# Weight conversion in 8 rounds with its last pass on GpSimd, and the first eight attention slots taken by token tile and turned on TensorE

## The chip, the cores and the metric

One core of a Trainium2 chip runs the whole kernel. The metric is device time in microseconds for one execution: 929.83 is the median of three runs of the kernel before, which lie between 923.97 and 930.18. The profile is of one more execution, timed at 926.31.

PE is the matrix engine (TensorE), DVE is VectorE, ACT is ScalarE, POOL is GpSimd, and SP is the engine whose queue issues most transfers. Matrix products land in PSUM, which GpSimd does not touch in this kernel; everything else is in the on-chip memory SBUF.

## What is computed

```python
scores = scale * np.matmul(q, k.transpose(0, 1, 3, 2))        # 8 batches, 8 heads, 576 x 576, depth 64
thresh = np.max(scores, axis=-1, keepdims=True) - tau
scores = np.where(scores >= thresh, scores, -1e9)
attn = exp(scores - max);  attn = attn / (sum(attn) + 1e-9)
x = matmul(attn, v)           # heads side by side: 4608 tokens x 512
h = x @ w_in                  # 512 x 1024
sm = softmax(h);  solu = h * sm
ln = (solu - mean) / sqrt(var + 1e-6) * g_ln
out = ln @ w_out              # 1024 x 512
```

q, k and v are 32-bit floats. The two weight matrices are 64-bit floats, and the kernel makes 32-bit floats of them with integer operations on the two words of each number.

## The kernel before, in words

**Slots and rounds.** A slot is one pair of heads with 128 queries of one batch. There are 18 slots to a batch: for each of two halves of the queries (`kind` 0 and 1) and each head pair `hp`, the two groups `r` of 128 queries; then two slots for the last 64 queries. The main loop runs one round per slot, 144 in all, and then some rounds of feed-forward alone. A round issues, in this order written out by hand, the scores of its slot on PE (L391, two PSUM tiles `s0`, `s1`, one for each head of the pair), the row maxima with the threshold on DVE (L408), the threshold ramp on ACT (L419), the exponentials with their sums on ACT (L428), and then for the slot before it `normalise` on GpSimd (L435 to L438: one over the sum, times each row) and `blocks` on DVE (L450: 32 x 32 block transposes into `T`). After both slots of a head pair four transfers on SP's queue (L461) bring the blocks into `wT`, and three or four rounds after that `attend` (L486) multiplies by v. Engines take their instructions in the order of issue, so what is issued later in a round stands behind what came earlier.

**Queries and keys.** q and k arrive with tokens on partitions. `whole_pair` turns one head pair of batch 0 with products by the identity into both PSUM tiles `p0` and `p1`, and six copies (`keep`, L297, L322, L338, L342) bring it to SBUF; it does so before round 0 and in rounds 0, 2 and 4. Later pairs are turned item by item in the spare columns of the score tiles. The keys are stored in an order of columns that suits the transposes of the weights (`k_parts`).

**Feed-forward.** When all head pairs of 256 tokens are attended, two tiles of 128 tokens become ready. A tile takes a cycle of four rounds, a quarter each: two halves of the first product (`ff_h`, L540, with a marker on GpSimd, `fence`, L106, between them), and in the next two the two halves of the second product (`ff_o`, L642) of the tile before. Between them come the softmax and the norm on ACT, DVE and GpSimd (L553 to L609), four transfers (L620) and a transpose on DVE (L630). The second product also waits until all weights are there (`w2_done`). Tiles 0 and 1 of batch 0 need slots 0 to 7, tiles 2 and 3 slots 8 to 15.

**Weights.** There are sixteen pieces of 128 x 512 numbers, eight of `w_in` and eight of `w_out`. In rounds 0 to 15 one piece is converted per round: the exponent (L216) and the mantissa (L222) are cut out on DVE, ACT puts the exponent in place (L221), and DVE then adds the low word (L236), puts in the sign (L239) and multiplies the two parts and the unit (L242). A piece of `w_out` is also copied with its partition halves exchanged (L251). Three buffers hold raw pieces; the next one is requested (L205) when its buffer's piece is done.

## Time and profile before

| | us |
|---|---|
| median of three runs | 929.83 |
| the profiled execution, as timed | 926.31 |
| its span | 924.5 |
| PE busy / DVE / ACT / POOL | 854.7 / 679.0 / 592.0 / 452.8 |
| L408, row maxima, mean of one | .755 |
| L428, exponential, mean of one | .772 |
| L438, scaling of one head's rows on GpSimd, mean of one | .771 |
| L436, reciprocal of the sums on GpSimd, mean of one | .745 |
| L236, L239, L242, passes of a weight piece on DVE | .656, .679, .692 to .752 |
| L216, L222, exponent and mantissa on DVE | .452, .479 |
| L221, exponent on ACT | .727 |

Busy times are sums over instructions of one engine; a mean is over all its instructions of that line. In the rows that the prediction shows, the first number of a row in order of time is its start from the beginning of the span and the second its duration, both in us; the square bracket says how long the engine was idle before it and what it waited for. In rows of groups the count stands after x, then the busy time in us and the mean of one in ns, then idle time before them. In the view of forty slices each digit is the busy share of a slice in tenths.

### The profile page before, as it was taken

The numbers are of one execution on the slowest core, as the hardware profiler recorded it, in microseconds if no ns is written. First come the engines' busy times: TensorE is split into PE (matmuls) and PEld (weight loads), VectorE is DVE, ScalarE is ACT, GpSimd is POOL, SyncE is SP. The second block draws the span as 40 slices with busy tenths as digits, with TensorE's granted clock in tenths as the row PEclk, the third lists the DMA queues.
The fourth block names the chain that finished last, engine by engine and source line by source line (L and its number), as shares of the span: only waits on it lengthen the run. The fifth ranks groups of instructions, "written<-read, shape, count | busy, mean of one in ns | idle before, by whom it ended". The sixth has DMA issues, their size and how long they took to land. (4 is left out here: it accounts for less than half of the span.)

```text
span 924.5 us, 39657 instructions
## 1 busy us (share of the span) xinstructions
PE 854.7 (92%) x17089; PEld 624.7 (68%) x17089; DVE 679.0 (73%) x1306; ACT 592.0 (64%) x1240; POOL 452.8 (49%) x870
## 2 busy tenths in 40 slices
PE   4657779989999999989997999999999999999997
...
DVE  4998967768867877767876777767877777877352
...
GB/s 244 200 260 261 186 124 198 229 179 124 187 169 224 128 140 185 237 150 134 184 183 209 94 136 182 229 150 130 186 185 224 121 131 128 191 145 140 90 47 47
DMA packets 95470, 154.61 MB, mean 167 GB/s; under 512 B 27192, under 2 KB 69184, under 8 KB 95296
## 3 DMA queue, kind: packets, MB, share of 16 engines
...
## 5 line engine op out<-in xcount | busy, mean ns | idle before, releaser
L408 DVE CUSTOM_DVE_ANT_0 w<-s_ps,tau_t 128x576 f32<-128x576 f32 x288 | 206.6, 755 | 157.2 <-PE s_ps L391 133.8
L419 ACT ACTIVATE w<-s_ps,nth 128x576 f32<-128x576 f32 x288 | 207.6, 744 | 127.1 <-DVE nth L408 106.2
L642 PE MATMUL o_ps<-w,uT 64*64 64x256 f32 x4608 | 271.2, 380 | 11.3 <-DVE uT L630 9.0
L642 PEld LDWEIGHTS o_ps<-w,uT 64*64 64x64 f32 x4608 | 221.6, 134 | 70.6 <-issue 27.9
L438 POOL TENSOR_SCALAR w<-w,sm 128x576 f32<-128x576 f32 x288 | 218.6, 771 | 14.3
L428 ACT ACTIVATE w<-w,ntau 128x576 f32<-128x576 f32 x288 | 220.3, 772 | 0.0
L540 PE MATMUL h_ps<-w,xh 64*64 64x512 f32 x1856 | 218.0, 591 | 0.7 <-issue 0.7
L450 DVE STREAM_TRANSPOSE T<-w 128x576 f32<-128x576 f32 x288 | 205.8, 751 | 4.5 <-POOL w L438 4.2
L486 PEld LDWEIGHTS pv<-wT,v 64*64 64x64 f32 x5760 | 168.0, 137 | 44.1 <-issue 24.7
L391 PE MATMUL s_ps<-kT,qT 64*64 64x64 f32 (+1 forms) x2048 | 173.2, 425 | 22.5 <-ACT w L419 19.0
L486 PE MATMUL pv<-wT,v 64*64 64x128 f32 (+1 forms) x5760 | 171.2, 265 | 10.8 <-DMA wT<-T 8.3
L540 PEld LDWEIGHTS h_ps<-w,xh 64*64 64x64 f32 x1856 | 110.1, 134 | 93.3 <-issue 67.9
L435 POOL TENSOR_SCALAR sm<-sm 128x2 f32<-128x2 f32 x144 | 36.1, 251 | 275.7 <-ACT w L428 272.9
L436 POOL TENSOR_TENSOR sm<-sm,mone 128x2 f32<-128x2 f32 x144 | 107.2, 745 | 12.0
L391 PEld LDWEIGHTS s_ps<-kT,qT 64*64 64x64 f32 x2048 | 64.1, 139 | 34.9 <-ACT w L419 24.9
L604 ACT ACTIVATE V<-u,nb,rs 128x1024 f32<-128x1024 f32 x36 | 44.7, 1241 | 53.2 <-POOL nb L594 53.2
L508 ACT COPY xh<-pv 128x256 f32<-128x256 f32 x64 | 23.9, 374 | 68.1 <-PE pv L486 68.1
L630 DVE STREAM_TRANSPOSE uT<-V 128x1024 f32<-128x1024 f32 x36 | 44.1, 1224 | 23.9 <-DMA V<-u 23.9
L562 ACT ACTIVATE u<-h_ps,hm 128x1024 f32<-128x1024 f32 x36 | 40.3, 1118 | 26.4 <-DVE hm L553 20.8
L428 ACT ACTIVATION_READ_ACCUMULATOR w<-w,ntau 128x1 f32 x288 | 57.0, 198 | 0.0
L553 DVE TENSOR_REDUCE hm<-h_ps 128x1 f32<-128x1024 f32 x36 | 43.0, 1195 | 9.4 <-PE h_ps L530 6.0
L568 DVE TENSOR_TENSOR u<-h_ps,u 128x1024 f32<-128x1024 f32 x36 | 42.8, 1189 | 9.6 <-ACT u L562 9.6
...
## 6 DMA issues: line engine op xcount, KB each, us to landing
wT<-T SPq DMA_DIRECT2D x288, 288.0 KB, 5.7
V<-u SPq DMA_DIRECT2D x144, 64.0 KB, 3.8
...
```

Of the source, the lines that this page charges most:

```text
L391: nc.tensor.matmul(out=ps[h][ROWS[y], ks], lhsT=lhsT, rhs=d["kT"][ROWS[h], ks], start=True, stop=True,)
L408: nc.vector.tensor_tensor_reduce(out=w, in0=ps[:, 0:S], in1=tau_t.to_broadcast([P, S]), scale=1.0, scalar=BIG, op0=ALU.add, op1=ALU.min, a ...
L419: nc.scalar.activation(out=d["w"][x], in_=d["ps"][x][:, 0:S], func=AF.Prelu, bias=d["nth"][x], scale=-1.0, alpha=1.0e30,)
L428: nc.scalar.activation(out=w, in_=w, func=AF.Exp, bias=ntau, scale=1.0, accum_out=sm[:, x : x + 1])
L436: nc.gpsimd.tensor_tensor(out=sm, in0=sm, in1=mone, op=ALU.pow)
L438: nc.gpsimd.tensor_scalar(out=w, in0=w, scalar1=sm[:, x : x + 1], scalar2=1.0, op0=ALU.mult, op1=ALU.mult)
L450: nc.vector.transpose(out=T[:, :, r, h, :], in_=w)
L486: nc.tensor.matmul(out=to, lhsT=d["v"][ROWS[u], h0 + h, m ^ 4 * u if m < 8 else m], rhs=rhs, start=m == 0, stop=m == NK - 1,)
L540: mm = nc.tensor.matmul(out=h[ROWS[y], f], lhsT=x[ROWS[r], c, ROWS[y]], rhs=w1_parts[ROWS[r], c, part ^ r], start=part == 0 and c == 0, st ...
L604: nc.scalar.activation(out=V, in_=u, func=AF.Identity, bias=nb, scale=rs)
L630: nc.vector.transpose(out=uT, in_=d["V"].rearrange("p y (m x) -> p m y x", x=32))
L642: nc.tensor.matmul(out=d["o"][ROWS[z], 512 * r : 512 * r + 256], lhsT=d["uT"][ROWS[r], m].rearrange("p y x -> p (y x)"), rhs=w2[ROWS[r], m ...
```

## The change

All sixteen weight pieces are converted in rounds 0 to 7, two per round. The pass that multiplies mantissa, unit and exponent moves from DVE to GpSimd, where it takes two instructions (`weight_d`). ACT's part of the two pieces stands before the ramps and between the two exponentials (`weight_b`), the sign pass and the next piece's first passes (`weight_c`, `weight_a`) in the middle and at the end of the round. Five raw buffers are used in place of three, and the first two pieces are requested on ACT's queue ahead of the constants.

The first eight slots run through the four head pairs for the first group of 128 queries and then for the second. Their weights are not scaled on GpSimd nor transposed on DVE: GpSimd multiplies the identity by one over each row's sum (`weigh`), PE multiplies the weights by this diagonal, which turns and scales them (`early_turn`), and copies on DVE, from round 4 on also on ACT, bring them to SBUF; the last 64 keys of both heads go through spare columns of a score tile. `early_attend` multiplies by v two rounds after a slot's scores, in the spare columns of the other score tile, so these slots use no transfer L461. For them the keys are kept in plain order, and `k_spread` on GpSimd makes the other order for the later slots. Token tile 0 is ready after slot 3, tile 1 after slot 7. `whole_pair` runs in rounds 0, 1 and 2, ahead of the exponentials.

```diff
--- before.py
+++ after.py
...
+    RAWS = ("xh2", "xh3", "uT", "u", "xh1")
+    def weight_load(x, queue):
         raw = work.tile(
-            [P, 512], I64 if wide else F32, tag=("xh2", "xh3", "uT")[x % 3], bufs=1, name="raw"
-        )
-        queue = nc.scalar if x < 3 else nc.sync
+            [P, 512], I64 if wide else F32, tag=RAWS[x % len(RAWS)], bufs=1, name="raw"
+        )
         queue.dma_start(out=raw, in_=piece(x)[0])
         raws[x] = dict(raw=raw)
...
+    def scratch():
+        ahead["two"] = two = work.tile([P, 2, DFF // 2], F32, tag="V", bufs=1, name="two")
+        ahead["kT"] = work.tile([P, NP, S], F32, tag="T", name="kT")
...
+    def load_ends():
+        for e in range(2):
+            nc.sync.dma_start(
+                out=ahead["ends"].rearrange("p (m e) d -> p m e d", e=2)[ROWS[e], :, e],
+                in_=v[0, :, SM:S, :].rearrange("(m e) p d -> p m e d", e=2)[:, :, e],
+            )
+    def words(x):
...
     def weight_a(x):
...
+        c = x - 2 * NP
+        if c < 0:
+            e, m = w2[:, 2 * x], w2[:, 2 * x + 1]
+        else:
+            e = w2[:, 2 * c + 1]
+            if c % 2:
+                m = ahead["two"][:, 1]
+            else:
+                m = work.tile([P, DFF // 2], F32, tag="xe", bufs=1, name="m")
+        e, m = e.bitcast(I32), m.bitcast(I32)
...
+        lo, hi = words(x)
         nc.vector.tensor_scalar(
             out=e, in0=hi, scalar1=20, scalar2=0x7FF,
             op0=ALU.logical_shift_right, op1=ALU.bitwise_and,
         )
-        nc.scalar.activation(out=e, in_=e, func=AF.Relu, bias=lim, scale=8388608.0)
         nc.vector.tensor_scalar(
             out=m, in0=hi, scalar1=0xFFFFF, scalar2=0x100000,
             op0=ALU.bitwise_and, op1=ALU.bitwise_or,
         )
-    def weight_b(x):
-        d = raws.pop(x)
-        _, dst, unit = piece(x)
-        if not wide:
-            nc.vector.tensor_scalar(out=dst, in0=d["raw"], scalar1=unit, scalar2=None, op0=ALU.mult)
-            return
-        words = d["raw"].bitcast(I32).rearrange("p (n two) -> p n two", two=2)
-        lo, hi = words[:, :, 0], words[:, :, 1]
-        e, m = d["em"]
         nc.vector.scalar_tensor_tensor(
             out=dst, in0=lo.bitcast(U32), scalar=2.0**-32, in1=m, op0=ALU.mult, op1=ALU.add
         )
-        nc.vector.scalar_tensor_tensor(
-            out=e, in0=hi, scalar=-(2**31), in1=e, op0=ALU.bitwise_and, op1=ALU.bitwise_or
-        )
-        nc.vector.scalar_tensor_tensor(
-            out=dst, in0=dst, scalar=unit, in1=e.bitcast(F32), op0=ALU.mult, op1=ALU.mult
-        )
+    def weight_b(x):
+        if wide:
+            e = raws[x]["e"]
+            nc.scalar.activation(out=e, in_=e, func=AF.Relu, bias=lim, scale=8388608.0)
+    def weight_c(x):
+        if wide:
+            e = raws[x]["e"]
+            nc.vector.scalar_tensor_tensor(
+                out=e, in0=words(x)[1], scalar=-(2**31), in1=e,
+                op0=ALU.bitwise_and, op1=ALU.bitwise_or,
+            )
+        if x + len(RAWS) < NW:
+            weight_load(x + len(RAWS), nc.sync)
     def weight_d(x):
+        _, dst, unit = piece(x)
+        d = raws.pop(x)
+        if wide:
+            nc.gpsimd.tensor_scalar(
+                out=dst, in0=dst, scalar1=unit, scalar2=1.0, op0=ALU.mult, op1=ALU.mult
+            )
+            nc.gpsimd.tensor_tensor(out=dst, in0=dst, in1=d["e"].bitcast(F32), op=ALU.mult)
         c = x - 2 * NP
         if c >= 0:
             for r in range(2):
@@ -305,6 +344,23 @@
         return n, make, keep
+    def k_plain(i):
+        return ahead["kT"][:, i]
+    def k_spread(i):
+        of = k_plain(i)
+        to = k_parts(i)
+        first = of[:, 0:SM].rearrange("p (t r k c) -> p r c t k", t=4, r=2, c=2)
+        for r in range(2):
+            nc.gpsimd.tensor_copy(
+                out=to[:, 4 * r : 4 * r + 4].rearrange("p t c k -> p c t k"), in_=first[:, r]
+            )
+        nc.gpsimd.tensor_copy(
+            out=to[:, NK - 1], in_=of[:, SM:S].rearrange("p (k c) -> p c k", c=2)
+        )
     def k_parts(i):
         return pair(i)["kT"].rearrange("p (c m k) -> p m c k", c=2, m=NK)
@@ -319,7 +375,12 @@
                 turn(spare, x + t, lambda r, y: src["k"][ROWS[r], h0 + y, ts.start + t])
         def keep(spare, x, r):
-            (nc.vector.tensor_copy if r and not spare.get("eased") else nc.scalar.copy)(
+            copy = nc.vector.tensor_copy if r and not spare.get("eased") else nc.scalar.copy
+            if i < NP:
+                plain = k_plain(i)[:, 0:SM].rearrange("p (t r k) -> p r t k", t=4, r=2)
+                copy(out=plain[:, r, ts], in_=seen(spare, r, x, n))
+                return
+            copy(
                 out=to[:, 4 * r + ts.start : 4 * r + ts.stop],
                 in_=seen(spare, r, x, n).rearrange("p t (k c) -> p t c k", c=2),
             )
...
@@ -364,8 +427,11 @@
             for hp in range(NP):
                 slots += [(b, kind, hp, 0), (b, kind, hp, 1)]
         slots += [(b, 2, 0, 0), (b, 2, 0, 1)]
+    EARLY = 2 * NP
+    slots[0:EARLY] = [(0, 0, hp, r) for r in range(2) for hp in range(NP)]
     live = {}
+    early = {}
     def scores(s, items):
         b, kind, hp, r = slots[s]
@@ -383,13 +449,15 @@
                 for y in range(2):
                     if kind < 2:
                         d = pairs[b * NP + hp]
+                        kT = k_plain(hp) if s < EARLY else d["kT"]
                         t = P * (2 * kind + r) + 64 * y
                         lhsT = d["qT"][ROWS[h], t : t + 64]
                     else:
                         d = pairs[b * NP + r + 2 * y]
+                        kT = d["kT"]
                         lhsT = d["qe"][ROWS[h]]
                     nc.tensor.matmul(
-                        out=ps[h][ROWS[y], ks], lhsT=lhsT, rhs=d["kT"][ROWS[h], ks],
+                        out=ps[h][ROWS[y], ks], lhsT=lhsT, rhs=kT[ROWS[h], ks],
                         start=True, stop=True,
                     )
         live[s] = dict(ps=ps, kept=kept, spare=spare)
@@ -425,6 +493,8 @@
         d = live[s]
         d["sm"] = sm = small.tile([P, 2], F32, tag="sm", name="sm")
         for x, w in enumerate(d["w"]):
+            if x and s < EARLY:
+                weight_b(2 * s + 1)
             nc.scalar.activation(
                 out=w, in_=w, func=AF.Exp, bias=ntau, scale=1.0, accum_out=sm[:, x : x + 1]
             )
@@ -461,6 +531,66 @@
                 nc.sync.dma_start(out=to[ROWS[half], g], in_=T[of : of + 32])
 
+    def weigh(s):
+        d = live[s]
+        sm = d["sm"]
+        nc.gpsimd.tensor_scalar(out=sm, in0=sm, scalar1=1e-9, scalar2=None, op0=ALU.add)
+        nc.gpsimd.tensor_tensor(out=sm, in0=sm, in1=mone, op=ALU.pow)
+        d["diag"] = diag = work.tile([P, 2, P], F32, tag="ob", name="diag")
+        for h in range(2):
+            nc.gpsimd.tensor_scalar(
+                out=diag[:, h], in0=ident, scalar1=sm[:, h : h + 1], scalar2=1.0,
+                op0=ALU.mult, op1=ALU.mult,
+            )
+    def early_turn(s, rnd):
+        d = live.pop(s)
+        tag, tp = take("tw")
+        last = live[rnd]["ps"][1][:, S : S + P]
+        for h in range(2):
+            w = d["w"][h]
+            for t in range(5):
+                if t < 4:
+                    o = 512 * h + P * t
+                    to, of = tp[:, o : o + P], w[:, P * t : P * t + P]
+                else:
+                    to, of = last[ROWS[h]], w[:, SM:S]
+                nc.tensor.matmul(out=to, lhsT=of, rhs=d["diag"][:, h], start=True, stop=True)
+        if s % 2 == 0:
+            early["wT"] = work.tile([P, 2, 9, P], F32, tag="wT", bufs=2, name="wT")
+        early[s] = wT = early["wT"][:, s % 2]
+        on_act = rnd > 3
+        nc.vector.tensor_copy(out=wT[:, 0:4], in_=tp[:, 0:512].rearrange("p (t k) -> p t k", t=4))
+        (nc.scalar.copy if on_act else nc.vector.tensor_copy)(
+            out=wT[:, 4:8], in_=tp[:, 512:1024].rearrange("p (t k) -> p t k", t=4)
+        )
+        (nc.scalar.copy if on_act else nc.vector.tensor_copy)(out=wT[:, 8], in_=last)
+        pairs_free.append(tag)
+    def early_attend(s, rnd):
+        b, kind, hp, r = slots[s]
+        wT = early.pop(s)
+        y = live[rnd]["ps"][0][:, S : S + P]
+        d, h0 = source(hp)
+        for t in range(5):
+            for h in range(2):
+                of = d["v"][:, h0 + h, t] if t < 4 else ahead["ends"][:, 2 * hp + h]
+                nc.tensor.matmul(
+                    out=y[ROWS[h]], lhsT=of, rhs=wT[:, 4 * h + t if t < 4 else 8],
+                    start=t == 0, stop=t == 4,
+                )
+        if hp == 0 and r == 0:
+            xh[0, 0] = work.tile([P, NP, 256], F32, tag="xh0", bufs=1, name="xh")
+        early["y"] = xh[0, 0][:, hp, P * r : P * r + P], y
+        if hp == NP - 1:
+            ready.append((rnd + 1, [(0, 0, r)]))
+    def early_attended():
+        if "y" in early:
+            to, y = early.pop("y")
+            nc.scalar.copy(out=to, in_=y)
     def attend(key):
         b, kind, hp = key
@@ -678,8 +808,8 @@
     pv_due = []
     for s, (b, kind, hp, r) in enumerate(slots):
-        if r == 1:
-            pv_due.append((s + LAG_PV + (s < 4), (b, kind, hp)))
+        if r == 1 and s >= EARLY:
+            pv_due.append((s + LAG_PV, (b, kind, hp)))
     def first_slot(i):
         return PER * (i // NP) + 2 * (i % NP)
...
@@ -709,19 +839,25 @@
     with tc.manual_schedule():
         load_qk(0, 0)
         nc.scalar.dma_start(out=tau_t, in_=tau.partition_broadcast(P))
+        for x in range(2):
+            weight_load(x, nc.scalar)
         constants()
-        for x in range(3):
-            weight_load(x)
+        scratch()
         load_qk(0, 1)
-        load_v(0, 0)
+        weight_load(2, nc.sync)
+        load_v(0, 0, (0,))
+        load_ends()
+        weight_load(3, nc.sync)
         nc.sync.dma_start(out=g_rows, in_=g_ln.rearrange("(c p) -> c p", p=P))
+        weight_load(4, nc.sync)
         whole_pair(0)
         weight_a(0)
 
-        pieces = {r: x for x, r in enumerate(range(16))}
-        whole = {0: 1, 2: 2, 4: 3}
-        load_at[3] = [lambda: load_v(0, 1)]
+        whole = {0: 1, 1: 2, 2: 3}
+        load_at[2] = [lambda: load_v(0, 1, (0,))]
+        load_at[6] = [lambda: load_v(0, 0, (1,))]
+        load_at[7] = [lambda: load_v(0, 1, (1,))]
         ready = []
         rnd = 0
@@ -771,16 +907,28 @@
                     items.append(make())
                     room -= n
                 scores(rnd, items)
+                if rnd - 2 in early:
+                    early_attend(rnd - 2, rnd)
                 maxes(rnd)
+                if rnd < EARLY:
+                    weight_b(2 * rnd)
                 ramp(rnd, 0)
                 keeps(rnd, 0)
                 keeps(rnd, 1)
                 ramp(rnd, 1)
+                early_attended()
+                if rnd < EARLY:
+                    weight_c(2 * rnd)
+                    weight_a(2 * rnd + 1)
+                if rnd in whole:
+                    whole_pair(whole[rnd])
                 exps(rnd)
-            if rnd in whole:
-                whole_pair(whole[rnd])
             if rnd - 1 in live:
-                normalise(rnd - 1)
+                (weigh if rnd - 1 < EARLY else normalise)(rnd - 1)
+            if 0 <= rnd - 1 < EARLY:
+                early_turn(rnd - 1, rnd)
+            if rnd < NP:
+                k_spread(rnd)
             for job in middle.pop(rnd, []):
                 job()
             due = bool(pv_due) and pv_due[0][0] <= rnd
@@ -843,16 +991,16 @@
                 job()
             if rnd == 3:
                 gains()
-            if rnd in pieces:
-                x = pieces[rnd]
-                weight_b(x)
-                if x + 3 < len(pieces):
-                    weight_load(x + 3)
-                if x + 1 < len(pieces):
-                    weight_a(x + 1)
-            if rnd - 1 in pieces:
-                weight_d(pieces[rnd - 1])
-                w2_done = pieces[rnd - 1] == NW - 1
+            if rnd < EARLY:
+                if rnd:
+                    weight_d(2 * rnd - 1)
+                weight_c(2 * rnd + 1)
+                if 2 * rnd + 2 < NW:
+                    weight_a(2 * rnd + 2)
+                weight_d(2 * rnd)
+            elif rnd == EARLY:
+                weight_d(NW - 1)
+                w2_done = True
             rnd += 1
```

`load_v` is split into the part that the early slots need and the part that they don't (the rows in exchanged halves), which is loaded in rounds 6 and 7. Two loads of batch 1 move by one round, from 12 and 15 to 11 and 14.

## The prediction

> **What bounds the kernel now.** I read the engine shares and the span in forty slices first, then the order of time in a conversion round, then the round starts on DVE. All durations are from one profiled execution (span 924.5 us, 926.31 us as timed, so 1.8 us around it; the three timed runs have median 929.83).
>
> ```profile
> PE 854.7 (92%) x17089; PEld 624.7 (68%) x17089; DVE 679.0 (73%) x1306; ACT 592.0 (64%) x1240; POOL 452.8 (49%) x870
> ...
> PE   4657779989999999989997999999999999999997
> ...
> DVE  4998967768867877767876777767877777877352
> ```
>
> A slice is 23 us. PE is full from the sixth slice on; only the first five, some 115 us, have slack worth having, and in the first three DVE is the full one. Round 9 shows why (order of time, DVE rows only, start and duration in us):
>
> ```profile
> 64.26 0.76 DVE L408 CUSTOM_DVE_ANT_0 w<-s_ps,tau_t 128x576 f32<-128x576 f32 x1 [0.26 <-PE s_ps L391]
> ...
> 65.62 1.43 DVE L450 STREAM_TRANSPOSE T<-w 128x576 f32<-128x576 f32 x2
> ...
> 66.98 0.65 DVE L236 SCALAR_TENSOR_TENSOR w<-raw,em 128x512 f32<-128x512 uint32 x1
> ...
> 67.55 0.68 DVE L239 SCALAR_TENSOR_TENSOR em<-raw,em 128x512 int32<-128x512 int32 x1
> ...
> 68.26 0.75 DVE L242 SCALAR_TENSOR_TENSOR w<-w,gs,em 128x512 f32<-128x512 f32 x1
> ...
> 68.93 0.42 DVE L216 TENSOR_SCALAR em<-raw 128x512 int32<-128x512 int32 x1
> 69.27 0.42 DVE L222 TENSOR_SCALAR em<-raw 128x512 int32<-128x512 int32 x1
> ...
> 69.60 0.75 DVE L408 CUSTOM_DVE_ANT_0 w<-s_ps,tau_t 128x576 f32<-128x576 f32 x1
> ```
>
> From 64.26 to 69.60 DVE never waits: maxima 1.36, two block transposes 1.36, one weight piece 2.6 us. Start to start, a piece is .34 + .34 + .6 + .7 + .65. Round 0 starts its maxima at 14.79, round 8 at 58.58, round 24 at 161.32 (first L408 row of each round). In the instruction order of the two programs, everything on PE after round 24's scores is the same list: tiles 0 and 1 of the feed-forward start at rounds 6 and 10 instead of 11 and 15, but tile 2 needs slot 15, which is not moved, and waits for it (round 20 against 19). So the filled PE time must show as an earlier round 24, or not at all. That start is what I predict.
>
> [...] in the conversion rounds pairs of L438 take 1.47 to 1.89 us, and L436, .72 at its shortest, often takes 1.28 beside DVE's two-input passes. [...] The granted clock between 20 and 25 us is .50, and twelve score matmuls take 2.19 us there against 1.19 in other rounds.
>
> **Part by part, in us.** M is the start of a round's maxima.
>
> *Start.* Weight pieces 0 and 1 are requested before the exponential table load. In the kernel before, piece 0 lands at 14.1 and DVE waits 3.6 for it; now its data is .5 MB behind about .9 MB on two queues, at 275 GB/s (5 to 10 us) I take 10.5. Then e, m and the low-word pass (1.4), and M0 is 12.3, when the cold scores are ready: 2.5 gained.
>
> *DVE.* A piece loses the last pass (L242): 2.1 with the wait for its own mantissa. Two pieces make 4.2. The two transposes go (-1.4). Copies of turned weights come from PSUM: 256 elements take .42 (L322 on DVE), so 512 take .62 to .69 and 128 take .2: 1.45 up to round 3, then .62 with the rest on ACT. Sum: 7.0 in rounds 1 to 3, 6.2 after, against 5.4, but eight rounds instead of sixteen.
>
> *GpSimd.* Removed: L438, 1.5 to 1.9. Added: two diagonals, 128 elements each, .33 by L438's slope (.7 the pair); two last passes, each a one-input pass of 512 (.68) and a two-input one [...]: 1.8 to 2.8 a piece with its waits, I take 2.4; three key copies in rounds 0 to 3, 1.2 to 1.8, taken at 1.4. With sum and reciprocal (1.6): 8.5 in rounds 1 to 3, 7.1 in 4 and 5. It was 3.2.
>
> *PE.* Added for each early slot: ten full-width multiplications by the diagonal, 20 passes. Nearest row:
>
> ```profile
> L530 PE MATMUL h_ps<-w,xh 128*128 128x512 f32 x48 | 21.7, 601 | 0.0
> ...
> L530 PEld LDWEIGHTS h_ps<-w,xh 128*128 128x128 f32 x48 | 8.8, 190 | 11.1 <-issue 10.3 <-DVE T L450 0.8
> ```
>
> These follow each other every .43 for 512 columns, .107 for 128; a weight load is .19. Fully hidden loads give 2.2, exposed ones 3.8, both halved clock 4.4 or more; I take 2.7. Attention, 20 passes in pairs of heads, is 1.15 a slot, as much as half of L486's 2.2 for two. The scores are 1.0 warm. PE runs in order: the turn of slot s-1 stands behind the scores of s and ahead of s+1, and waits for GpSimd's diagonal. Scores of s+1 also wait for the copies from the borrowed tail of the score banks.
>
> *DMA.* The 4 L461 transfers of four early units, 288 KB each, go (4.6 MB). Weight loads double in rate, .5 MB each with five buffers instead of three, requested some 2.5 rounds ahead, 18 us against a landing time of 7 to 9; cost nothing unless DMA bandwidth (the slices show up to 261 GB/s) is short. On SP a load waits for DVE's sign pass and holds back the v loads behind it; these are needed rounds later.
>
> *Rounds.* Round 0: ramps end at 2.2; six keeps of pair 1 (1.95); exp (.75); Relu of the second piece (.7): 5.6; then sign pass and next piece, 2.1: **7.7**. Rounds 1 and 2: pair 2 or 3 takes both PSUM banks, so the turn waits for its keeps: 2.2 + 1.45 + turn 2.7 + copies .85 + 2.1: **9.3 each**. Round 3: DVE alone, **7.15**. Rounds 4 and 5: DVE 6.2, GpSimd 7.1 with slack from before: **6.7 each**. Rounds 6 and 7 hold the first feed-forward halves (3.4 each), and GpSimd's fence marker (L106) stands behind the first half and ahead of the last passes and the next diagonal: 1.8 until the diagonal, 2.7, 3.4, then 4.8 for two pieces and 2.3 for sum and diagonal, 2.7, 3.4, 1.0 for scores, .9 on DVE: **23**. Rounds 8 and 9, no feed-forward, turns of the last slots: **10.2**. Sum 80; round 10 starts at 92.3.
>
> *Rounds 10 to 23*, by the same kinds of rounds before: a first half 4.6 (147.47 to 152.04), an o half 4.2 (to 156.21), with key items 5.1 (to 161.32), no step 4.0 (round 0 to 1): 5.6, 4.6, 4.2, 5.5, three attention rounds at 4.8, 4.2, 5.4, 4.2, 7.3, 4.6, 4.0, 4.4, sum 68.4. Here the old kernel's wait of 5.46 for the swap at 119 is gone. Round 24 starts at 160.7, **.6 earlier** than 161.3. That is 925.7 by the profiled execution, 929.2 by the median; I give **927**, between.
>
> **Rivals.** (1) *The engines overlap* (chance .20, 915). If turns hide behind DVE in rounds 1 and 2 and GpSimd's passes run uncontended, round 8 starts at 67.4 (12.3 + 5.4 + 3 x 6.9 + 2 x 6.2 + 2 x 8.3), and rounds 10 to 23 could fall to 64 where PE alone limits: 142, 20 less. Half of this, 10 to 12, gives 915. For it: PE is idle some 40 of the first 115 us. Against: four engines are near 7 us a round with waits across them. (2) *GpSimd becomes the bound* (.25, 937; slower). With 3.0 a piece, 2.6 for sum and diagonal, 1.8 for keys, rounds 1 to 3 take 10.4 and rounds 4 and 5 8.6: 2.2 + 3.2 + 3.8, and 1.8 in the fenced rounds, 11 in all with L436's 1.28 as usual. It decides from 2.35 a piece, where GpSimd's mean over rounds 1 to 5 (2.3 + .84 + two pieces) passes the 7.8 of my sum; that is close. A cold clock on the turns adds 5. (3) *The lead is given back* (.55, 919 to 935): my case; the resynchronisation at round 24 throws away any order gained, and only time counts.
>
> **Numbers.** Range: the fast rival down to 913, the slow one to 941. A difference of about 1% (9.3 us) is what a measurement of this kernel can tell: faster is below 920.5, most of rival 1 and a little of mine; slower is above 939.1, the upper half of rival 2 and a cold clock.
>
> **What would show it.** Round starts at 12.3, 20, 29, 39, 46, 52, 59 and 82 (round 8), 92 (round 10), 161 (round 24). L106's marker followed by 7 us of GpSimd before PE's next turn. GpSimd at seven tenths or more in the first three slices, DVE with gaps behind PE's turn in rounds 1 and 2. The prediction fails if a two-input GpSimd pass of 512 is under 1 or above 1.9, if full-width turns take over 3.5, if DVE's own passes stretch beside GpSimd, or if rounds 10 to 23 stall on the swap's transfers again.

## The result: 3.7% slower, and the profile after

The kernel after takes 961.1 us (median of four runs, 957.7 to 962.2) against 926.9 (922.1 to 930.2) for the kernel before: the ratio is 1.037, with an interval of 1.031 to 1.043. The prediction was 927, next to no change, with a range of 913 to 941. The measured time lies above the whole range, above its slow rival too. The profiled execution has a span of 955.7 us against 924.5, 31.2 more. All ratios leave out executions over 1.5% above the fastest of their kernel (one of four of last_pass_dve, loads_early and filler each), and medians keep them.

The profile page of the kernel after, first engine shares, then the span in forty slices (24 us each):

```profile
PE 884.2 (93%) x17121; PEld 675.6 (71%) x17121; DVE 675.3 (71%) x1286; ACT 595.4 (62%) x1256; POOL 478.5 (50%) x915
...
PE   3776898798999999999999999989999999999997
...
DVE  4675585676887777668777777757877777888352
...
POOL 3764553554655555444555555545555555565220
PEclk9688898999999999999999999989999999999999
```

In the first four slices no engine is full any more: before, DVE showed 9 9 8 from the second on; now DVE shows 6 7 5, PE 7 7 6 and GpSimd (POOL) 7 6 4, its only seven. Where nobody is full and time is lost, engines wait for each other.

The round starts (first row-maximum instruction of a round on DVE, L408 before, L476 after) say where. PE's list of products after the scores of round 24 is the same in both programs, so the start of round 24 had to carry the effect. It does: 194.35 us against 161.32, 33.0 later; what follows takes 761.4 us against 763.2.

| us | before | predicted | after | after less predicted |
|---|---|---|---|---|
| start of round 0 | 14.79 | 12.3 | 14.29 | +2.0 |
| round 0 | 3.95 | 7.7 | 7.22 | -.5 |
| rounds 1 and 2 | 11.38 | 18.6 | 26.69 | **+8.1** |
| round 3 | 5.35 | 7.15 | 10.06 | **+2.9** |
| rounds 4 and 5 | 12.15 | 13.4 | 20.30 | **+6.9** |
| rounds 6 and 7 | 10.96 | 23 | 25.66 | +2.7 |
| rounds 8 and 9 | 11.02 | 10.2 | 11.95 | +1.8 |
| rounds 10 to 13 | 28.95 | 19.9 | 20.43 | +.5 |
| rounds 14 to 16 | 23.15 | 14.4 | 21.61 | **+7.2** |
| rounds 17 to 23 | 39.62 | 34.1 | 36.14 | +2.0 |
| start of round 24 | 161.32 | 160.7 | 194.35 | +33.6 |

Round 4 after is the pattern that I had not seen. Some rows of all engines, in order of time:

```profile
57.82 0.39 PE L580 MATMUL s_ps<-wT,two 128*64 128x128 f32 x4
...
58.26 0.76 DVE L476 CUSTOM_DVE_ANT_0 w<-s_ps,tau_t 128x576 f32<-128x576 f32 x1 [1.65 <-PE s_ps L580]
...
60.45 1.32 POOL L286 TENSOR_TENSOR w<-w 128x512 f32<-128x512 f32 x1 [2.05 <-DVE w L271]
...
60.53 0.43 PE L560 MATMUL s_ps<-diag,w 128*64 128x128 f32 x2 [1.23 <-ACT w L487]
60.56 1.50 DVE L253 TENSOR_SCALAR two<-raw 128x512 int32<-128x512 int32 x1
...
61.98 0.43 PE L560 MATMUL s_ps<-diag,w 128*64 128x128 f32 x2
...
62.77 0.68 DVE L565 COPY wT<-tw 128x512 f32<-128x512 f32 x1
...
63.97 0.27 ACT L569 COPY wT<-s_ps 128x128 f32<-128x128 f32 x1
...
64.30 2.14 PE L459 MATMUL s_ps<-kT,qT 64*64 64x64 f32 x12 [1.62 <-ACT wT L569]
...
66.36 1.77 PE L580 MATMUL s_ps<-wT,v 128*64 128x128 f32 x16
...
68.41 0.76 DVE L476 CUSTOM_DVE_ANT_0 w<-s_ps,tau_t 128x576 f32<-128x576 f32 x1 [2.88 <-PE s_ps L580]
```

This is a ring, a loop in which each step waits for the one before and the last one lets the first start again. It runs through the score tiles, because the early slots borrow spare columns of the two tiles that the scores are in. Its four legs are:

1. Maxima and ramps, 2.27 us. The maxima (58.26) wait not for the scores but for `early_attend` (L580), which writes into the same tile.
2. The rest of the turn, 1.88. Head 0's product for the last 64 keys goes into the other tile and waits until ACT's ramp has read it (PE idle for 1.23 us), and head 1's products stand behind it in PE's order.
3. The copies, 1.89. Most of the next scores wait until the last copy out of that tile is done (L569), with PE idle for 1.62 us.
4. Scores and product with v, 4.11. The twelve score products take 2.14 us, and 1.19 elsewhere: they run at half clock.

The sum is 10.15 us, and no engine is full in it. The half clock of the fourth leg shows in these stretches: their length, the busy times of PE, weight loads, DVE, ACT and GpSimd, then the granted clock, DMA share and GB/s.

```profile
57.60:64.40 6.80, 3.94 (x40) 2.98 (x40) 6.04 (x12) 4.46 (x10) 3.49 (x6) 1.00 0.26 80
64.40:67.80 3.40, 3.40 (x26) 1.79 (x28) 1.02 (x2) 0.72 (x1) 3.32 (x5) 0.50 0.74 230
67.80:74.60 6.80, 3.95 (x40) 2.98 (x40) 6.09 (x12) 4.49 (x11) 3.38 (x5) 1.00 0.43 120
74.60:78.00 3.40, 3.40 (x28) 1.79 (x26) 0.97 (x2) 0.69 (x1) 1.31 (x2) 0.50 1.12 243
```

Such a stretch starts 10.2 us after the one before, so the half clock meets the scores and the product with v again in the next round.

Rounds 2, 6 and 7 have the waits of which the prediction had spoken, at a higher price. From the order of time of the kernel after:

```profile
38.04 2.04 PE L560 MATMUL tw<-diag,w 128*128 128x128 f32 x8 [2.84 <-ACT kT L405]
...
40.64 2.08 PE L560 MATMUL tw<-diag,w 128*128 128x128 f32 x8
...
42.75 0.69 DVE L565 COPY wT<-tw 128x512 f32<-128x512 f32 x1 [3.81 <-PE tw L560]
...
86.40 0.10 POOL L106 MEMSET mark<- 128x1 f32 x1 [10.49 <-PE h_ps L670]
86.47 0.69 POOL L283 TENSOR_SCALAR w<-w,gs 128x512 f32<-128x512 f32 x1
...
92.10 1.06 POOL L542 TENSOR_SCALAR diag<-ident,sm 128x128 f32<-128x128 f32 x2
...
92.86 2.07 PE L560 MATMUL tw<-diag,w 128*128 128x128 f32 x8 [4.33 <-POOL diag L542]
```

In round 2 the turn waits for the last of six copies of the new head pair, and eight products take 2.04 instead of the 1.16 that they take at full clock; DVE idles 3.8 us behind them. In round 6 GpSimd waits 10.5 us at the marker for the first feed-forward half, then has four weight passes before the diagonal of round 7, and PE waits 4.33 us for that.

### The profile page after: what moved, and what is told of

The parts are those of the page before. It is cut to its first block, busy times and chain, and to the rows that moved or that the text cites. A ratio compares the mean times of both kernels' runs of the same rounds, so it can differ in the third digit from the quotient of the medians.

```text
span 955.7 us, 39761 instructions
## 1 busy us (share of the span) xinstructions
PE 884.2 (93%) x17121; PEld 675.6 (71%) x17121; DVE 675.3 (71%) x1286; ACT 595.4 (62%) x1256; POOL 478.5 (50%) x915
## 5 line engine op out<-in xcount | busy, mean ns | idle before, releaser
L476 DVE CUSTOM_DVE_ANT_0 w<-s_ps,tau_t 128x576 f32<-128x576 f32 x288 | 206.8, 755 | 182.2 <-PE s_ps L459 139.3
L772 PEld LDWEIGHTS o_ps<-w,uT 64*64 64x64 f32 x4608 | 230.6, 133 | 51.4 <-issue 11.1
L670 PE MATMUL h_ps<-w,xh 64*64 64x512 f32 x1856 | 225.2, 601 | 0.3 <-issue 0.3
L508 POOL TENSOR_SCALAR w<-w,sm 128x576 f32<-128x576 f32 x272 | 205.3, 767 | 13.5
L459 PE MATMUL s_ps<-kT,qT 64*64 64x64 f32 (+1 forms) x2048 | 180.1, 420 | 25.1 <-DVE kT L405 4.8
L520 DVE STREAM_TRANSPOSE T<-w 128x576 f32<-128x576 f32 x272 | 194.5, 751 | 5.4 <-POOL w L508 5.3
L616 PEld LDWEIGHTS pv<-wT,v 64*64 64x64 f32 x5472 | 161.8, 134 | 33.8 <-issue 23.3
L670 PEld LDWEIGHTS h_ps<-w,xh 64*64 64x64 f32 x1856 | 122.6, 136 | 87.8 <-issue 47.9
L616 PE MATMUL pv<-wT,v 64*64 64x128 f32 (+1 forms) x5472 | 163.1, 261 | 9.8 <-issue 6.0
L506 POOL TENSOR_TENSOR sm<-sm,mone 128x2 f32<-128x2 f32 x136 | 96.7, 711 | 11.3
L459 PEld LDWEIGHTS s_ps<-kT,qT 64*64 64x64 f32 x2048 | 69.5, 137 | 29.3 <-ACT qe L399 4.9
```

Source lines behind the costliest of these rows:

```text
L459: nc.tensor.matmul(out=ps[h][ROWS[y], ks], lhsT=lhsT, rhs=kT[ROWS[h], ks], start=True, stop=True,)
L476: nc.vector.tensor_tensor_reduce(out=w, in0=ps[:, 0:S], in1=tau_t.to_broadcast([P, S]), scale=1.0, scalar=BIG, op0=ALU.add, op1=ALU.min, a ...
L506: nc.gpsimd.tensor_tensor(out=sm, in0=sm, in1=mone, op=ALU.pow)
L508: nc.gpsimd.tensor_scalar(out=w, in0=w, scalar1=sm[:, x : x + 1], scalar2=1.0, op0=ALU.mult, op1=ALU.mult)
L520: nc.vector.transpose(out=T[:, :, r, h, :], in_=w)
L616: nc.tensor.matmul(out=to, lhsT=d["v"][ROWS[u], h0 + h, m ^ 4 * u if m < 8 else m], rhs=rhs, start=m == 0, stop=m == NK - 1,)
```

## Experiments

All are edits of the kernel after unless something else is said. Times are medians; ratios are to the kernel before, run beside them on the same chip (926.0 to 927.5 us).

### The two parts, each alone

**turns_alone** keeps the early slots and turns, but converts one piece per round.

```diff
-    RAWS = ("xh2", "xh3", "uT", "u", "xh1")
+    RAWS = ("xh2", "xh3", "uT")
...
-                if rnd < EARLY:
-                    weight_b(2 * rnd)
+                if rnd < NW:
+                    weight_b(rnd)
...
+            if rnd < NW:
+                weight_c(rnd)
+                if rnd + 1 < NW:
+                    weight_a(rnd + 1)
+                weight_d(rnd)
...
-                ready.append((rnd + 1, [(0, 0, r)]))
+                ready.append((11 + 4 * r, [(0, 0, r)]))
```

> The part of the change that concerns the first eight slots (token tiles, the diagonal, turns on PE, products with v in the score tiles), with the weights at one piece per round in rounds 0 to 15, three raw buffers, and the feed-forward from round 11 as in the kernel before; the last pass stays on GpSimd. Theory A: the ring of the early slots doesn't need the second weight piece: rounds 3 to 6 keep 8.5 to 10 us each, against 5.3 to 6.9 before; rounds 0 to 9 take 85 to 95, rounds 10 to 23 what they take before (97) or a few less: time 935 to 955. Theory C (two pieces a round are what makes the rounds long): rounds 3 to 6 fall to 6 to 7 us and the time to 915 to 930.

Measured: 947.1 us, ratio 1.023 (1.019 to 1.027). Rounds 1 and 2 took 12.45 and 13.70 us; round 3 took 8.39 and rounds 4 to 8 took 7.84 or 7.85 each; rounds 0 to 9 took 84.6. Busy times in rounds 5 and 6, by engine:

```profile
58.99:66.84 7.85, 5.74 (x56) 3.90 (x56) 5.18 (x10) 4.57 (x10) 4.07 (x7) 1.00 0.23 77
66.84:74.68 7.84, 5.74 (x56) 3.89 (x56) 5.18 (x9) 4.57 (x10) 4.06 (x7) 1.00 0.59 149
```

The fullest engine, PE, is busy 5.74 of 7.85 us, at full clock: the ring needs no second piece, and it has a length of its own of 7.85 us. By the rows of round 6 its legs add up to that: 2.27 from the maxima to the end of the ramp, 1.88 for the rest of the turn, 1.21 for three copies, one behind the other, 1.12 for scores, 1.36 for the product with v. Theory A was right in kind; rounds 3 to 6 all came below its 8.5 to 10.

**conversion_alone** keeps the conversion in eight rounds and gives slots, scaling, block transposes and the loads of v back to the form before.

```diff
-    slots[0:EARLY] = [(0, 0, hp, r) for r in range(2) for hp in range(NP)]
...
-                (weigh if rnd - 1 < EARLY else normalise)(rnd - 1)
-            if 0 <= rnd - 1 < EARLY:
-                early_turn(rnd - 1, rnd)
-            if rnd < NP:
-                k_spread(rnd)
+                normalise(rnd - 1)
```

> The other part alone: sixteen pieces in rounds 0 to 7, two per round, last pass on GpSimd, with the slots, the scaling, the block transposes and the transfers of the kernel before. Theory A: with no ring a round is DVE's own work, 4.2 us of weights, 1.4 of maxima, 1.4 of transposes, 7 to 7.5 us, so round 8 starts at 70 to 76; rounds 8 to 15 without weights fall from 6.1 to 4.5 or 5: round 24 starts at 152 to 162, time 917 to 930. Theory C (two pieces a round, through DVE and GpSimd, make the rounds long): rounds 3 to 6 take 9 to 10 us, round 8 starts at 85 or later, and the time is 940 or more.

Measured: 944.5 us, ratio 1.019 (1.014 to 1.025); rounds 3 to 6 took 9.25 to 9.29, round 8 started at 85.8. Theory C was right here. Busy times and two rows of round 5:

```profile
60.20:69.49 9.29, 3.51 (x32) 1.24 (x25) 9.22 (x15) 4.52 (x9) 7.73 (x9) 0.50 1.00 262
```

```profile
62.76 1.31 POOL L283 TENSOR_TENSOR w<-w 128x512 f32<-128x512 f32 x1 [0.69 <-DVE w L268]
62.87 1.49 DVE L250 TENSOR_SCALAR two<-raw 128x512 int32<-128x512 int32 x1
```

DVE is busy 9.22 of 9.29 us. By its own durations in the kernel before it should have 7.0: two pieces at 2.1, maxima 1.4, transposes 1.4. The mantissa pass, .42 us long elsewhere, takes 1.49: it started .1 us behind GpSimd's two-input pass and ended .29 behind that pass's end. The rounds without weights, 8 to 15, gave little back: 51.2 us against 52.6 before. In round 10, which took 14.0 instead of 9.2, PE was idle for 6.2 us for the transfers wT<-T.

**conversion_dve** is conversion_alone with the last pass on DVE.

```diff
-            nc.gpsimd.tensor_scalar(
-                out=dst, in0=dst, scalar1=unit, scalar2=1.0, op0=ALU.mult, op1=ALU.mult
-            )
-            nc.gpsimd.tensor_tensor(out=dst, in0=dst, in1=d["e"].bitcast(F32), op=ALU.mult)
+            nc.vector.scalar_tensor_tensor(
+                out=dst, in0=dst, scalar=unit, in1=d["e"].bitcast(F32), op0=ALU.mult, op1=ALU.mult
+            )
```

> As conversion_alone (sixteen pieces in rounds 0 to 7, attention as before), but the last pass of a piece is one instruction on DVE again. With GpSimd's passes DVE was busy 9.2 us of each 9.29 us round. If DVE's own passes were stretched by GpSimd's two passes beside them (mantissa 1.49 and .89 instead of .42, low word 1.05, sign pass .98 to 1.06 instead of .68): DVE has 1.5 us more to do and yet a round takes 8.3 to 8.7, and round 24 starts 3 to 6 us earlier than 180.7. If the stretch has another cause (the saturated DMA engines, or the two pieces themselves), a round takes 10 to 10.8 us and the time is longer by 5 to 8 us.

Measured: 942.3 us, ratio 1.018 (1.014 to 1.022); rounds 2 to 6 took 8.22 to 8.84, and round 24 started 3.2 us earlier than in conversion_alone. That is as expected for passes stretched by GpSimd; the two whole times are too close to be told apart. The DMA engines are as full as there (share .99 to 1.07 in rounds 3 to 5, and .96 to 1.01 in conversion_alone), so they aren't what stretches the passes. The groups of the mantissa pass on DVE in this kernel:

```profile
L250 DVE TENSOR_SCALAR w<-raw 128x512 int32<-128x512 int32 x8 | 3.3, 417 | 0.0
...
L250 DVE TENSOR_SCALAR m<-raw 128x512 int32<-128x512 int32 x4 | 1.7, 419 | 0.0
L250 DVE TENSOR_SCALAR two<-raw 128x512 int32<-128x512 int32 x4 | 1.7, 416 | 0.0
```

and in conversion_alone:

```profile
L250 DVE TENSOR_SCALAR w<-raw 128x512 int32<-128x512 int32 x8 | 7.5, 940 | 0.0
...
L250 DVE TENSOR_SCALAR two<-raw 128x512 int32<-128x512 int32 x4 | 6.0, 1490 | 0.0
...
L250 DVE TENSOR_SCALAR m<-raw 128x512 int32<-128x512 int32 x4 | 3.6, 888 | 0.0
```

All groups of DVE's four other weight passes together (L246, L250, L254, L268) are 52.7 us with GpSimd's passes and 37.9 without; the last pass on DVE costs 12.6. So **moving the last pass to GpSimd made DVE's weight work longer, 52.7 us against 50.5**: the passes that stayed lost 14.8 us, more than the pass that left had cost. What makes a pass on one engine hold up a pass on the other is not shown by a run here; the traces show the time, with the .29 us above. The move cost VectorE 2.2 us.

**last_pass_dve** makes the same edit in the kernel after.

> The changed kernel with the last pass of each weight piece on DVE again, as one instruction of .75 us, in place of two on GpSimd; all else as it is. Theory A (the ring of waits through the score tiles, with DVE idle 2.9 us ahead of the maxima of each such round): GpSimd's part does not matter; DVE's 1.5 us more per round fit its idle time in part, and the mantissa pass falls from 1.5 to .45 where GpSimd's two-input pass was beside it: rounds 3 to 6 between 9.7 and 10.8, time 957 to 966. Theory B (GpSimd is what holds these rounds up): rounds 3 to 6 fall to 8 or less and the time to under 950.

Measured: 953.4 us, ratio 1.026 (1.021 to 1.031). Round 3 took 10.28, rounds 4 and 5 7.85 and 7.88, round 6 10.00, round 7 10.88 instead of 15.64. Neither theory had this. The busy times of rounds 4 and 5 in the kernel after (first fence, rounds 3 to 5) and in last_pass_dve (second):

```profile
48.20:58.26 10.06, 7.41 (x58) 4.82 (x59) 8.27 (x17) 4.43 (x9) 6.43 (x8) 0.83 0.32 108
58.26:68.41 10.15, 7.29 (x57) 4.72 (x58) 7.06 (x14) 5.18 (x11) 6.75 (x9) 0.83 0.42 129
68.41:78.56 10.15, 7.30 (x57) 4.73 (x58) 7.05 (x13) 5.18 (x11) 4.08 (x6) 0.83 0.70 167
```

```profile
56.03:63.88 7.85, 5.67 (x57) 3.90 (x58) 7.40 (x16) 5.18 (x11) 3.08 (x4) 1.00 0.34 110
63.88:71.76 7.88, 5.70 (x57) 3.93 (x58) 7.43 (x17) 5.18 (x11) 3.40 (x5) 1.00 0.58 158
```

DVE has more to do (7.40 against 7.06), and the round is 2.3 us shorter: it has fallen back to the ring's own 7.85, and the granted clock is 1.00 instead of .83. GpSimd is busy only 4 to 7 us of 10 in the kernel after, so it isn't the bound. The order of time in round 5 of last_pass_dve (its line numbers are one lower from L475 on) shows what became of the rows of the ring:

```profile
63.88 0.76 DVE L475 CUSTOM_DVE_ANT_0 w<-s_ps,tau_t 128x576 f32<-128x576 f32 x1
...
66.18 0.42 DVE L253 TENSOR_SCALAR two<-raw 128x512 int32<-128x512 int32 x1
...
67.71 0.69 DVE L564 COPY wT<-tw 128x512 f32<-128x512 f32 x1 [0.38 <-PE tw L559]
...
69.24 1.19 PE L458 MATMUL s_ps<-kT,qT 64*64 64x64 f32 x12 [0.95 <-ACT wT L568]
```

The mantissa pass takes .42 again instead of 1.50, so the first copy of turned weights starts 3.83 us after the maxima and not 4.51; PE's gap ahead of the scores is .95 and not 1.62 us, and the scores then run at full clock. So GpSimd's pass acts through DVE: it makes the copies .7 us later, and the other 1.6 us of the round are the scores and the product with v at half clock, behind the longer gap: 7.85 + .7 + 1.6 = 10.15. This is a second form of theory A; the filler below tests its clock part.

### The ring taken apart

**ring_loosened** puts the product with v behind the turn and the 64-key products at the turn's end.

```diff
-        for h in range(2):
+        for h, t in [(h, t) for h in range(2) for t in range(4)] + [(0, 4), (1, 4)]:
             w = d["w"][h]
-            for t in range(5):
...
-                if rnd - 2 in early:
-                    early_attend(rnd - 2, rnd)
                 maxes(rnd)
...
                 early_turn(rnd - 1, rnd)
+            if rnd - 2 in early:
+                early_attend(rnd - 2, rnd)
+                early_attended()
```

> The changed kernel with another order in the first ten rounds: the product with v of an early slot stands behind the turn of the next one instead of ahead of the row maxima, and the two 64-key products of a turn come after both heads' eight. Theory A (the early rounds are a ring of waits through the borrowed columns of the score tiles: the maxima wait 2.1 us for the product with v, head 1's turn waits .5 to 1.2 for ACT's ramp): rounds 3 to 6 fall from 10.1 us each to 8 to 9, round 10 starts 8 to 14 us earlier than its 116.2, and the time is 947 to 954. Theory B (GpSimd's last pass of the weights, and what it does to DVE beside it, bounds these rounds): rounds 3 to 6 stay within .5 us of 10.1 and the time within 3 us of 961.

Measured: 948.2 us, ratio 1.024 (1.020 to 1.028). Rounds 3 to 6: 9.40, 8.44, 7.46, 9.60; round 7, with its fence, 16.89; round 10 started at 106.0, 10.2 us earlier, of which 2.6 are an earlier start of round 0. The four rounds take 34.9 us instead of 40.4, so the waits that the order of instructions sets are real and theory A has the sign and most of the size (it expected 8 to 9 for each). Which of the two edits gave how much is not shown, as they were made together; round 4 still ran in part at half clock (.64).

**pairs_apart** keeps the old order of slots, so that a new head pair is turned every second round, and turns it behind the weights (its `k_spread` moves with it).

```diff
-    slots[0:EARLY] = [(0, 0, hp, r) for r in range(2) for hp in range(NP)]
...
                 early_turn(rnd - 1, rnd)
+            if rnd in whole:
+                whole_pair(whole[rnd])
...
-        whole = {0: 1, 1: 2, 2: 3}
+        whole = {0: 1, 2: 2, 4: 3}
```

> The changed kernel with the first eight slots in the old order (both groups of 128 queries of a head pair, then the next pair), so that a new pair is turned in rounds 0, 2 and 4 and not in 0, 1 and 2, and behind the turn of weights instead of ahead of it. Theory A: rounds 1 and 2 took 12.6 and 14.1 because the turn of the weights waits for the six copies of the new pair out of both PSUM pairs, and then runs at half clock: round 1 falls to 9 to 10, round 2 to 9 to 10.5, round 4 grows by up to 2; token tile 0 starts two rounds later. Round 10 starts 6 to 10 us earlier than 116, the time is 950 to 956. If the cold turns or the two weight pieces alone make these rounds long: rounds 1 and 2 stay above 12.

Measured: 949.5 us, ratio 1.024 (1.017 to 1.030); round 1 took 11.77, round 2 9.43, round 4 9.88, round 10 started at 102.2. Round 2 is 4.7 us shorter, but at a granted clock of 1.00 instead of .64, and in three other kernels whose round 2 is that of the kernel after (loads_early, swap_on_act and filler) it took 10.80 to 10.85 at clock 1.00. So the wait for the copies of the new pair is worth some 1.4 us there and the clock 3.3. For round 1 the wait was not the cause (.8 less). There the diagonal comes at 20.2 us, PE has then been idle 3.5 us and runs at a granted clock of .56 through turn, scores and product, and GpSimd is busy 10.95 of 11.77 us. But with less on GpSimd and more on DVE, in last_pass_dve, the round was no shorter (13.12), so GpSimd alone is not its bound, and what is the bound stays open.

**filler** and **filler_half** add products that nobody reads, behind the turn in rounds 3, 4 and 5: twelve and six.

```diff
+                if rnd in (3, 4, 5):
+                    fill()
...
+    def fill():
+        tag, t = take("fill")
+        for x in range(12):
+            nc.tensor.matmul(
+                out=t[:, 0:P], lhsT=ident, rhs=ident, start=True, stop=True
+            )
+        pairs_free.append(tag)
```

> The changed kernel with PE work added that nobody reads: in rounds 3, 4 and 5, behind the turn, twelve products of the identity by itself (128 columns, .145 us each, 1.7 us at full clock) into the PSUM pair that the turn doesn't use. Theory A, in its second form (the ring is 7.85 us long at full clock, as with the last pass on DVE, and 10.1 with the scores and the product with v at half clock, which the 1.6 us idle time ahead of the scores brings about): with that idle time filled the rounds from 4 to 6 fall from 10.15 to between 7.9 and 8.9 us each, although PE has more to do; the time falls by 3 to 6 us. If the half clock is an effect and not a cause, or the added work delays the scores: these rounds stay at 10.1 or grow up to 11.8.

> The changed kernel with six products of the identity by itself in rounds 3, 4 and 5 behind the turn, nobody reads them: twelve passes, 1.5 us at full clock by the filler with twelve products (24 passes, 2.94 us), where scores wait 1.6 us in the changed kernel. If the half clock that follows this gap costs rounds 4 and 5 1.5 to 2 us each: these take 8.2 to 8.8 us instead of 10.15, less than with the filler of twelve (9.45), whose last .9 us held the scores up. If the half clock costs nothing: 10.0 to 10.3.

Measured: rounds 4 and 5 of filler took 9.45 each, at a granted clock of 1.00:

```profile
54.63:64.08 9.45, 7.38 (x75) 5.62 (x74) 7.05 (x15) 5.18 (x11) 6.61 (x8) 1.00 0.41 140
64.08:73.53 9.45, 8.22 (x81) 6.46 (x82) 7.05 (x13) 5.18 (x11) 4.76 (x7) 1.00 0.71 180
```

Those of filler_half took 9.66 and 8.52:

```profile
54.60:64.26 9.66, 7.39 (x61) 5.57 (x62) 7.05 (x14) 5.18 (x11) 6.81 (x9) 0.82 0.40 134
64.26:72.78 8.52, 7.20 (x69) 5.31 (x70) 7.06 (x13) 5.18 (x11) 4.58 (x6) 1.00 0.54 163
```

The rounds of filler are .7 us shorter than in the kernel after **with 2.9 us of work added** on PE, on a ring whose other parts are the same; the sixteen score products took 1.21. It missed the expected 7.9 to 8.9 because each product shows on PE as two (x24 for the twelve of round 5, 2.94 us in all), so the filler was 2.94 us and not 1.7, and ended 1.0 us after the copy for which the scores wait. With half of it, round 5 took 8.52 at clock 1.00, as expected, and round 4 9.66 at .82, which missed: there turn and filler ran at half clock. So the half clock is a cause, worth about 1.6 us a round. The traces of loads_early, swap_behind and swap_on_act, with no filler and the same instructions in these rounds, agree: their rounds 4 and 5 took 8.91 to 10.23 us, and the two shortest, 8.91 and 9.62 in loads_early, are those in which the scores ran at full clock.

The whole times are another matter: 961.8 us, ratio 1.036 (1.028 to 1.043), and 969.9, ratio 1.049 (1.043 to 1.055). Round 24 started 5.4 and 1.1 us earlier than in the kernel after, but 2.3 us of that are an earlier start of round 0 in both, so filler_half had gained nothing by then; and what follows round 24's start took 11 to 12 us longer. The list of PE's waits, kernel after and filler_half, columns total, times and longest:

```profile
PE pv L616 <- issue: 6.0, 4, 2.3
...
PE s_ps L459 <- issue: 4.7, 3, 3.0
```

```profile
PE s_ps L459 <- issue: 15.2, 5, 4.5
```

"Issue" is idle time for which the profile shows no wait. Summed over all of PE's lines it is 8.7 us before, 13.9 after, 17.3 in filler and 27.9 in filler_half, in stalls of up to 4.5 us. The traces show what the longer ones have in common. All ten such stalls over .6 us in the kernel after end 1.3 to 1.9 us after a transfer of the queue that the page calls "q8 instruction" has ended, and all five before, all eleven of filler and all twelve of filler_half end within 1.2 to 2.0 us of one; of all instructions of PE only about one in ten starts at such a distance. No run changes this alone, so it isn't shown that these transfers cause the stalls. Behind the start of round 24 the stalls of filler and filler_half are 6 and 8 us longer than those of the kernel after, which leaves some of the 11 to 12 us open.

### Rounds 10 to 23

**loads_early** asks for the second batch's q, k and v in rounds 9 and 10.

```diff
-            (2, 8, 9) if b > 1 else (8, 11, 14), (load_qk, load_qk, load_v), (0, 1, 0)
+            (2, 8, 9) if b > 1 else (8, 9, 10), (load_qk, load_qk, load_v), (0, 1, 0)
```

> The changed kernel with the loads of the second batch (q and k of its second four heads, v of its first four) in rounds 9 and 10 instead of 11 and 14. Theory D (the 7.2 us lost in rounds 14 to 16 are the transfers of turned weights, L531, queued on SP behind these loads and behind saturated DMA engines): rounds 14 to 16 fall from 21.6 us to 15 to 17, round 24 starts 4 to 7 us earlier, time 954 to 958. If PE's products themselves, at the clock of that stretch, set these rounds: no change, within 1 us in these rounds.

Measured: 952.3 us, ratio 1.028 (1.025 to 1.031), but not for the reason named: rounds 14 to 16 took 20.5 us instead of 21.6. Theory D fell. In the profiled execution the gain is in the start (2.0 us) and in rounds 0 to 7, whose instructions are those of the kernel after: 83.6 us instead of 89.9. Round 2 had a granted clock of 1.00 and took 10.84, where the kernel after had .64 and 14.13. The same rounds took 88.4 in swap_behind and 88.0 in swap_on_act, below. So a part of the loss in rounds 1 to 5 changes from one execution to the next; why the same instructions met different clocks is not shown by a run here. Why three executions of loads_early (950.8 to 952.5 us) all lie below the four of the kernel after, while swap_behind with the same loads does not, stays open.

**swap_behind** is loads_early with the transfers V<-u of the first tiles behind wT<-T, and **swap_on_act** is loads_early with V<-u on ACT's queue.

```diff
-                middle.setdefault(rnd + 3, []).append(lambda t=cur: (ff_norm2(t), ff_swap(t)))
+                middle.setdefault(rnd + 3, []).append(lambda t=cur: ff_norm2(t))
+                (late if rnd < 20 else middle).setdefault(rnd + 3, []).append(lambda t=cur: ff_swap(t))
```

```diff
+        queue = nc.scalar if at < 20 else nc.sync
...
-                nc.sync.dma_start(
+                queue.dma_start(
                     out=d["V"][to : to + 32, 1 - g],
```

> The kernel with the loads of the second batch in rounds 9 and 10, and besides the four transfers V<-u of the first tiles (those that start before round 20) issued behind the block transposes and the transfers wT<-T of their round instead of ahead of them. With the loads alone the product with v of round 16 still waited for wT<-T, which stood behind V<-u on SP's queue, and rounds 14 to 16 took 20.5 us. If that order in the queue is the rest of what rounds 14 to 16 lose: they fall to 15 to 17.5 us, and round 24 starts 3 to 5 us earlier than 185.6 less the difference of the starts. If PE's own work sets them: 20 us or more, no gain, or a loss where the second product waits for V.

> The kernel with the second batch's loads in rounds 9 and 10, and the transfers V<-u of the tiles that start before round 20 issued on ACT's queue, so that V<-u and wT<-T no longer stand behind each other. If the one in-order queue on SP is what rounds 14 to 16 lose: they fall from 20.5 to 15.5 to 18 us and round 11 stays at 5, rounds 10 to 23 take 72 to 75 us instead of 77.2. If PE's work, or ACT, which now waits for the norm on DVE before it goes on, sets them: 20 us or more, rounds 10 to 23 at 76 to 80.

Measured: swap_behind 961.5 us, ratio 1.037 (1.031 to 1.043); rounds 14 to 16 took 19.8 us, and round 11 took 10.9 instead of 5, with PE waiting 5.4 us for the turned V. swap_on_act 958.6 us, ratio 1.037 (1.030 to 1.043): rounds 14 to 16 took 21.1, round 11 6.7, and PE waited 3.6 us for a copy on ACT. Both missed. Each order gives the wait to another round. Rounds 10 to 23 took 77.2 to 83.5 us in all eight kernels with this order of feed-forward and tiles, so the 7 us lost in rounds 14 to 16 stay without one cause; in the kernel after PE is busy 67.0 of the 78.2 us, and 3.3 us of the rest are two "issue" stalls of L616 in rounds 14 and 15, which end 1.5 and 1.4 us after an instruction transfer.

### Start, and what the runs point to

**before_early_raw** is the kernel before with the change's early request for two weight pieces.

```diff
+        for x in range(2):
+            weight_load(x)
         constants()
-        for x in range(3):
-            weight_load(x)
+        weight_load(2)
```

> The kernel before with one thing of the change: the first two weight pieces are requested on ACT's queue ahead of the constants. The maxima of round 0 start at 11.4 to 12.5 us instead of 14.8 (the changed kernel and three of its variants have 11.4 to 14.3). If the early rounds, which DVE fills, carry this to round 24: that starts at 158 to 159.5 instead of 161.3 and the time falls by 2 to 3 us, a ratio of .997. If the waits of rounds 10 and 16 (9.2 and 10.5 us) swallow it: round 24 at 161, no difference.

Measured: 929.3 us, ratio 1.005 (.998 to 1.011): no difference. Round 0 started at 13.45 instead of 14.79, round 24 at 160.6 instead of 161.3; rounds 5, 6, 10 and 15 are longer. Of a lead of 1.3 us .7 are left there, and the time shows nothing of it.

**rearranged** joins ring_loosened, pairs_apart, last_pass_dve and loads_early, and copies the 64-key part first. Two of these take a part of the change back: the order of the slots and the last pass on GpSimd. **rearranged_swap** and **rearranged_act** add the two edits of V<-u.

```diff
-        on_act = rnd > 3
+        on_act = rnd in (1, 3) or rnd > 4
+        nc.vector.tensor_copy(out=wT[:, 8], in_=last)
         nc.vector.tensor_copy(out=wT[:, 0:4], in_=tp[:, 0:512].rearrange("p (t k) -> p t k", t=4))
```

> The changed kernel put together anew from what the first runs say: product with v behind the turn, 64-key products last and their copy first, last pass of the weights on DVE, one new head pair every second round behind the turn instead of one in each of rounds 0 to 2 ahead of it, loads of the second batch in rounds 8 to 10. Theory A (a ring of waits on the score tiles and PSUM pairs, which lets PE idle and so run at half clock): rounds 1 and 2 fall from 12.6 and 14.1 to 8 to 9, rounds 3 to 7 to 7.4 to 8, round 8 starts at 70 to 76 and round 24 at 153 to 164: time 917 to 931. If turning eight slots on PE beside two pieces a round is bound otherwise, rounds stay at 9 or more, round 24 comes after 172 and the time is above 938.

> The rearranged kernel (931 us) with the transfers V<-u of the first tiles behind wT<-T. There PE was busy 72 of the 80 us of rounds 10 to 23, so at most the rest is to be had. If the wait for wT<-T at 131 us goes (1.9 us): round 24 starts at 163 to 165 instead of 166, time 927 to 931, no difference from the kernel before that three rounds can tell. If PE's own work sets this stretch: no change within 1 us.

> The rearranged kernel with the transfers V<-u of the first tiles on ACT's queue. PE is busy 72 us of the 80 in rounds 10 to 23 there. If the queue holds it up: rounds 10 to 23 take 75 to 78 us, time 926 to 930, level with the kernel before. If PE's work sets it: 79 to 81, time as the rearranged kernel's within 2 us.

Measured: 931.1 us, ratio 1.004 (.999 to 1.008); 931.9, ratio 1.007 (1.004 to 1.010); 930.5, ratio 1.005 (1.003 to 1.008). Rounds 1 and 2 of rearranged took 9.46 and 8.13, rounds 3 to 7 7.44, 8.20, 7.60, 7.59 and 6.37; round 8 started at 72.9 instead of 104.2, round 24 at 166.2 instead of 194.4. Round 24 came 2 us later than the 164 that theory A allowed. Of the 28 us gained there 2.7 are an earlier start of round 0; from there to round 24 it is 154.5 us, against 180.1 in the kernel after and 146.5 before. So 25.5 of 33.5 us come from the five edits. Rounds 10 to 23 keep 79.9 us there, with PE busy for 72.2, and the edits of V<-u change nothing: most of this stretch is PE's. No form beat the kernel before. PE's busy time up to round 24 points to why: 113.7 us before, 129.6 in rearranged, 144.4 in the kernel after. The rearranged change still adds 16 us to it, where the clock is mostly full (.93 over rounds 0 to 9); the 15 us more in the kernel after come with a granted clock of .83 there.

## Why the prediction was wrong, point by point

The step that failed is the price of an early round as the sum of its fullest engine, 6.7 us in rounds 4 and 5. The runs showed a ring of waits in its place: 7.85 us at full clock, .7 more because DVE's passes stretch beside GpSimd, and 1.6 more at half clock. Rounds 1 to 5 are 17.9 of the 33.6 us by which round 24 was missed. Another 9.8 lie in rounds 10 to 23, and their cause stays open.

- **Start.** Predicted 12.3, measured 14.29. It spreads: variants with this early request have 11.4 to 14.4. In the kernel after the first wait of DVE, for `tau`, ended at 10.45 us, in last_pass_dve at 7.6, so the first transfers make a part of it. The lead of 2.5 us was .5, and a lead of that kind is of no use (before_early_raw).
- **Round 0**: 7.7 against 7.22, right.
- **Rounds 1 and 2, "9.3 each": failed (+8.1).** The wait of the turn for the copies was named and is there (4.91 and 2.84 us). The turn behind it, taken at 2.7, was 5.2 and 5.3 at half clock; in round 2 the scores and part of the product with v followed at half clock, in round 1 they had the full one. I had 4.4 or more as the bound at half clock and let it decide nothing but the range of a rival. Six traces with the same instructions in these two rounds took 23.4 to 26.7 us, so of the 8.1 at least 4.8 are missing in each.
- **Round 3, "DVE alone", and rounds 4 and 5, 6.7: failed (+9.8).** I added up engines and took the longest; the round is set by a ring of waits through the borrowed columns, 7.85 us at full clock and 10.15 with the gap and the half clock. I had written that the scores wait for the copies from the borrowed tail, and gave it no time. That the maxima wait for `early_attend`, and head 1 for ACT's ramp, I had missed.
- **DVE 7.0 and 6.2 a round: failed.** It was 8.27 in round 3 and 7.06 in round 4, for passes that stretch beside GpSimd (the mantissa pass took 1.50 us there, and .42 in last_pass_dve). I named this as a way to fail, but priced it on GpSimd's side alone. (The first DVE slices also lie one later than I read them: the 9 9 8 are slices 2 to 4, and PE's first 9 is the seventh slice.)
- **GpSimd, 2.4 a piece: nearly right**, 2.0: .68 and 1.28 to 1.37, in the mean. The 2.4 was an estimate: the two-input passes on GpSimd in the kernel before have one or two numbers a row, so its trace gives no price for 512. The bounds for that pass, 1 and 1.9, held (1.26 to 1.59). By the prediction's own sums (8.5 on GpSimd against 7.15 in round 3, and 2.4 a piece against the 2.35 from which it decides) GpSimd would have been the bound by about .5 us in all, which I passed over. It isn't the bound in rounds 3 to 5, so rival 2 had the sign and not the mechanism.
- **Rounds 6 and 7**: 23 against 25.66; the fence is as described, with a turn at half clock (2.07 and 2.08 us for eight products each). In last_pass_dve they took 20.9. **Rounds 8 and 9**: 10.2 against 11.95.
- **Attention, 1.15 a slot**: 1.3 at full clock, 2.0 as it ran. **Turn, 2.7**: 2.9 at full clock. **Scores, "1.0 warm"**: 1.5 at full clock, with their 64-key products.
- **Rounds 10 to 23: failed (+9.8)**, in the three attention rounds at 4.8 (21.6 instead of 14.4). Rounds 10 to 13 were right to .5 us. The 4.8 had no room for waits, and the runs show waits that move from one round to another.
- **"DMA costs nothing"**: right in rounds 3 to 5, at a share of .32 to .70. **Round 24 carries the effect**: right; but my case that the lead is given back presumed a lead.
